# Another order of the loads ahead of and in the first 17 steps of an attention and two-layer-MoE kernel on one core

## The chip, the cores and the metric

The kernel runs on one core of one Trainium2 chip. The metric is the device time of one execution in microseconds (us); lower is better. The core has TensorE (PE, matrix products), VectorE (DVE), ScalarE (ACT), GpSimd (POOL) and SyncE (SP), which here only issues transfers. Each engine works through its own list of instructions in the order in which the program gave them, and waits at an instruction until what it needs is there.

## What is computed

```python
scores = scale * (q @ k.T)                       # 4 batches, 8 heads, 576 tokens, head size 64
scores = where(mask, scores, -1e9)               # 4 heads local (32 back), 4 heads strided (every 32nd)
x = softmax(scores) @ v                          # -> 2304 tokens x 512
h = x @ w_in;  x = (h * cos(h)) @ w_out          # first MoE layer, 512 -> 2048 -> 512
h = x @ w_in2                                    # second layer, the same sizes
g = (a0 + a1*h + a2*h**2 + a3*h**3) / (1 + |b0|*|h| + |b1|*h**2 + 1e-6)
out = g @ w_out2
```

The weights come as 64-bit floats and are decoded on the chip.

## The kernel before

**Work and tiles.** Attention is cut into 8 halves `n` (batch and half of its tokens) by 4 pairs of heads `pr`. The first layer runs over 5 blocks of tokens (512, 352, 480, 480, 480 columns), each in 16 steps, one for each 128-wide slice `f` of the hidden layer; that makes steps 0 to 79. The second layer runs over 5 blocks of 384 or 512 tokens, steps 80 to 159. In step `g`, `l1` (L478) makes `h` for its slice with 12 matmuls, ACT and DVE make `h*cos(h)` of it (letters U or u, V, N, M, G, H or h of `ew_op`), and `l2` (L495) adds the slice of step `g-2` into the output banks `y` with 12 matmuls (9 or 12 in the second layer). Each product is made of a high and a low part: `w_split` makes a weight tile's high part (ACT, L260) and its low part (DVE or POOL, L263); `att_oe` (L456, L457) does the same for attention's result, `xh` and `xl`.

**The start.** The halves 0 and 1 of attention are computed ahead of step 0, in the order of the list START, a line for each piece: `lq` and `lv` load q with k, and v; `load i j` loads a weight tile (a `raw` of 128 x 1024 words, 512 KB); `s` scores; `red` and `exps`, or `ms` and `ex`, two ways to the softmax (`exps` is five ACTIVATE with their sums, `ex` a single one); `t`, `te`, `o`, `oe` transpose, copy, multiply by v, split; `abs`, `d`, `split` decode a weight tile (ACT L233, L238; DVE L248, L250, L252, L254) and split it. A command has its engine or bank behind it.

**Queues.** Loads go through the queue of SP, a few of START through that of ACT. An issue waits until the transfer eight places before it in the program has landed, and until its buffer is free; all behind it in that queue wait too.

**The steps.** The other halves of attention ride along with steps 0 to 63. PAIR tells for each of them (key -4 is half 2, pair 0) the steps of: load q, load v, scores, masked maximum, exp, sum and reciprocal, transpose, product with v. W1LD tells the step whose end loads the weight tiles of pairs 6 to 15 of the first layer. The decoding of pair k begins in step k-3. ORD[g] is the order, letter by letter, of what ACT, DVE and POOL get in step g. W2T tells when a tile of the second layer's weights is decoded and stored back to memory; W2RD tells how many steps after step 64+f the two tiles of slice f, read back, are split (the third number is how many steps earlier they are read).

```python
            if g < N1:
                run("pe", g)                      # attention's matmuls of this step, behind l1
                for c in order(g): ...            # ORD[g]
                second(g, LAG)                    # l2 of step g-2
            run("load", g)                        # loads of this step, behind all of it
```

Of the kernel before, what the change touches and what calls it, by code (L numbers as in the profile page):

```python
# [88 lines left out]
ORD = {0: 'UVNykMaz1bpqGsHW23O4E',
 1: 'U1VSOyENz2MWb34aGpkqh',  # L90
 2: 'SOUEwzVNbyq1MaGkH234p',
 3: 'ykUzVwEN1SbOaMqp23G4h',
 4: 'Ey1USakVzwNbM2pGqO3H4',
 5: 'Uk1VwSObNMzy2q3EGaph4',
 6: 'yuVWskzN1ME2pqabGOH34',
 7: 'zUVwSN1yaMkp23EqObG4h',
 8: 'O1sUVwEzkNMaqGbH2y34p',
 9: 'UsH1OVy2bEWzap3G4qNMk',
 10: 'UkEbVyWGz1pNOM2q34has',
 11: 'yUsVN1az2EM3WGkOHqbp4',  # L100
 12: 'zb1ywkOG23SEUaMV4pqNh',
 13: 'UzaMVys1bqpE23NOW4kGH',
 14: 'byE1UpzMks2a3VOqNWG4H',
 15: 'zk1SMypUVObwGaHN234qE',
 16: 'Ud1EMkeVGO2r3Nfi4H',
 17: 'udekOfiMVGrEN12h34',
# [19 lines left out]
 37: 'kUVENM1dGhefOi234r',  # L126
 38: 'kUVE1NMdGOefi23h4r',
 39: 'kUVENMdG1Oefi23h4r',
 40: 'kUVENM1dGOefi234hr',
 41: 'kUVENM1OdGefi234hr',  # L130
 42: 'kUVENM1OdGefi234hr',
# [9 lines left out]
 52: 'UMdkV1ENGef2Hi34rO',
 53: 'MdkUVN1EGef23rHi4O',
 54: 'UVMk1dENGefi2H34rO',
 55: 'kuVM1dENGefi2h34rO',
 56: 'kuVM1dENGefi2h34rO',
 57: 'kuVM1d2ENGefih34rO',
 58: 'kuVM1d2ENGefih34rO',
 59: 'kuVM1d2ENGefih34rO',
 60: 'kuVM1d2ENGefih34rO',
 61: 'kuVM1dENGef2hO34ri',  # L150
 62: 'uVENM1kdGefiO234Hr',
 63: 'kuVM1dNGeEfi2HO34r',
# [9 lines left out]
 73: 'kUEV1MdNGefO2i3hr4',
 74: 'kUEV1MdNGefO2i3hr4',
 75: 'kUEV1MdNG2efOi34hr',
 76: 'kUEV1MGNdef2i34hrO',
 77: 'kUEV1MGNOdefi234hr',
 78: 'kU1MVNdEOGefi234Hr',
 79: 'UMNVEd1kOGefi234hr'}
START = ['cst ACT', 'lq 0 0 ACT', 'lq 0 1', 'lq 0 3 ACT', 'lv 0 0 ACT', 'lv 0 3 w0 ACT', 'lv 0 2 w0', 'lq 1 1 w1', 'lq 0 2 ACT', 'lq 1 0 w1', 'lq 1 3 w1 ACT', 'lq 1 2 w1 ACT', 'lv 1 0 w0 ACT', 'load 0 0',
# [777 lines left out]
```

## Time and profile before

| | us |
|---|---|
| three runs, median (lowest to highest) | 922.94 (922.39 to 923.59) |
| the profiled execution, its own time | 923.4 |
| its span, first to last instruction | 921.6 |
| PE busy in it | 891.8 (97%) |
| DVE busy | 661.9 (72%) |
| ACT busy | 624.5 (68%) |
| POOL busy | 239.1 (26%) |

A timeline row has its start, its duration, engine, line of the kernel, instruction, tile written and tiles read, and in brackets how long the engine had been idle and what released it. Matmuls overlap: a row of one lasts longer than the distance to the next.

### The profile page before, as it was taken

What the parts mean: (1) busy time and instruction counts of PE and PEld (TensorE: products, weight loads), DVE (VectorE), ACT (ScalarE), POOL (GpSimd) and SP (SyncE); (2) the same over time, 40 slices, a digit from 0 to 9 for tenths busy, and PEclk for the clock granted to TensorE, in tenths of its full rate; (3) what the DMA queues carried; (4) which work ended last, traced back from release to release, by engine and by line L of the source; (5) the groups of instructions that cost most, each with busy time, mean ns of one, the idle gap of its engine ahead of it and who ended that gap; (6) DMA issues with size and microseconds to landing.
All of it is one profiled execution on the core that took longest, in us unless ns stands there. A gap on an engine that the chain in (4) does not pass through costs nothing.

```text
span 921.6 us, 14207 instructions
## 1 busy us (share of the span) xinstructions
PE 891.8 (97%) x5263; PEld 760.9 (83%) x5263; DVE 661.9 (72%) x1162; ACT 624.5 (68%) x1106; POOL 239.1 (26%) x203
## 2 busy tenths in 40 slices
PE   8599999999999999999999999999999999999998
PEld 7477777999888887888888889888888888888986
DVE  5689985767685665576356798777777677767776
ACT  4789976667557555423355889777777777777775
POOL 0133553221321112201221124233223322332221
PEclk9799999999999999999999999999999999999999
DMA  9983041665644444231323340020011002000100
GB/s 274 325 280 135 8 154 56 203 206 163 185 131 155 154 120 147 95 109 51 97 87 116 102 131 1 1 80 1 0 53 40 1 1 80 1 1 1 46 1 35
DMA packets 54677, 88.16 MB, mean 96 GB/s; under 512 B 9544, under 2 KB 30800, under 8 KB 54608
## 3 DMA queue, kind: packets, MB, share of 16 engines
q1 hardware_dynamic: 51596, 83.64, 28.5%
q10 hardware_dynamic: 3012, 3.62, 1.3%
...
## 4 chain that ended last, share of the span: by engine, by line
PE 81%; DMA 7%; ACT 6%; DVE 4%; issue 1%; SPq 0%; ACTq 0%; POOL 0%; DVEq 0%
PE y L495 39%; PE h L478 27%; PE a L478 10%; DMA raw<-in_w_dram 3%; PE a L335 2%; DMA v<-in_vv_dram 2%; PE a L443 2%; PE a L421 1%; DMA qk<-in_qk_dram 1%; DMA ab<-in_a_dram 1%; ACT dec L233 1%; DVE w L263 1%; ACT w L260 1%; ACT gh L570 1%; ACT raw L238 1%
## 5 line engine op out<-in xcount | busy, mean ns | idle before, releaser
L478 PE MATMUL h<-xh,w 128*128 128x480 f32 (+3 forms) x960 | 296.6, 370 | 4.2 <-ACT w L260 2.6
L495 PE MATMUL y<-gh,w 128*128 128x480 f32 (+2 forms) x640 | 205.0, 382 | 0.0
L478 PEld LDWEIGHTS h<-xh,w 128*128 128x128 f32 x960 | 178.9, 188 | 30.0 <-DVE u L567 2.9
L495 PE MATMUL y<-w,gh 128*128 128x512 f32 x576 | 190.7, 390 | 1.3 <-ACT ev L510 1.3
L478 PE MATMUL h<-xl,w 128*128 128x480 f32 (+3 forms) x480 | 178.5, 372 | 0.0
L537 POOL TENSOR_TENSOR z<-q,r 128x512 f32<-128x512 f32 (+1 forms) x80 | 94.7, 1184 | 279.8 <-ACT r L536 276.9
L495 PEld LDWEIGHTS y<-gh,w 128*128 128x128 f32 x640 | 120.3, 190 | 18.6 <-issue 0.3
L495 PEld LDWEIGHTS y<-w,gh 128*128 128x128 f32 x576 | 108.1, 188 | 23.7 <-ACT ev L510 1.6
L495 PE MATMUL y<-gl,w 128*128 128x480 f32 (+2 forms) x320 | 119.9, 375 | 0.2 <-DVE gl L572 0.2
L495 PE MATMUL y<-w,gl 128*128 128x512 f32 x288 | 113.0, 392 | 0.7 <-DVE gl L550 0.5
L526 DVE SCALAR_TENSOR_TENSOR q<-q,z 128x512 f32<-128x512 f32 (+1 forms) x80 | 52.7, 659 | 84.4 <-ACT z L524 84.4
L478 PEld LDWEIGHTS h<-xl,w 128*128 128x128 f32 x480 | 90.6, 189 | 13.0
L478 PE MATMUL a<-xh,w 128*128 128x512 f32 (+1 forms) x320 | 98.2, 367 | 0.0
L565 ACT ACTIVATE u<-u,biases 128x480 f32<-128x480 f32 (+2 forms) x80 | 54.4, 680 | 61.3 <-DVE u L563 60.3
L559 ACT ACTIVATE u<-h,biases 128x480 int32<-128x480 f32 (+2 forms) x64 | 40.9, 638 | 78.9 <-PE h L478 78.9
L563 DVE SCALAR_TENSOR_TENSOR u<-h,u 128x480 f32<-128x480 f32 (+2 forms) x80 | 50.9, 636 | 55.1 <-ACT u L559 54.2
L572 POOL TENSOR_TENSOR gl<-u,gh 128x480 fp32r<-128x480 f32 (+2 forms) x31 | 40.5, 1306 | 147.4 <-ACT gh L570 130.4
L495 PEld LDWEIGHTS y<-gl,w 128*128 128x128 f32 x320 | 61.0, 191 | 8.5 <-DVE gl L572 0.7
L478 PEld LDWEIGHTS a<-xh,w 128*128 128x128 f32 x320 | 59.4, 188 | 8.1
L495 PEld LDWEIGHTS y<-w,gl 128*128 128x128 f32 x288 | 54.1, 188 | 12.7 <-DVE gl L550 2.2
L570 ACT ACTIVATE gh<-u 128x480 fp32r<-128x480 f32 (+2 forms) x80 | 46.2, 577 | 20.8 <-DVE u L567 20.6
L478 PE MATMUL a<-xl,w 128*128 128x512 f32 (+1 forms) x160 | 59.1, 369 | 0.0
(126 smaller groups left out, 1455.0 us busy)
## 6 DMA issues: line engine op xcount, KB each, us to landing
...
```

The lines of the kernel that those rows point to most:

```text
L233: ACT.activation(out=m, in_=src, func=AF.Copy, scale=2.0 ** -112)
L335: PE.matmul(sv[r, i], t[r, q0:q0 + D], rhs[r], start=not mask, stop=not mask or i == nb - 1)
L443: PE.matmul(o[64 * j:64 * j + 64, q * i:q * i + m], v[0:w, i, 64 * j:64 * j + 64], r[i][0:w, 64 * j:64 * j + m], start=True, stop=True)
L478: PE.matmul(h[:, :n], w[d["ph"], f, 0][:, 128 * c:128 * c + 128], x[c][:, cs], start=k == 0, stop=k == len(ops) - 1)
L495: PE.matmul(y, l, r, start=first and i == 0, stop=last and i == 2)
L526: DVE.scalar_tensor_tensor(out=q, in0=q, scalar=1.0 + 1e-6, in1=z, op0=ALU.add, op1=ALU.add)
L537: POOL.tensor_tensor(out=z, in0=q, in1=r, op=ALU.mult)
L559: ACT.activation(out=k, in_=h, func=AF.Identity, scale=INV_2PI, bias=biases[:, 2:3])
L563: DVE.scalar_tensor_tensor(out=u, in0=h, scalar=INV_2PI, in1=k, op0=ALU.mult, op1=ALU.subtract)
L565: ACT.activation(out=u, in_=u, func=AF.Sin, scale=TWO_PI, bias=biases[:, 3:4])
L570: ACT.activation(out=e["gh"], in_=u, func=AF.Copy)
L572: (POOL if c == "H" else DVE).tensor_tensor(out=e["gl"], in0=u, in1=e["gh"].bitcast(F32), op=ALU.subtract)
```

## The change

It replaces the tables: START, PAIR, W1LD, W2RD, W2T, ORD, the two default orders AB_ORD and C_ORD, and M3 (one more weight tile is decoded with two DVE instructions in place of one on DVE and one on ACT). A new table WHE sends both parts of four splits of the second layer's weights to named engines. No transfer, no matmul and no tile is added or taken away; in START six sets of scores instead of four go through `red` and `exps`.

```diff
-W2RD = (5, 7, 2)
+W2RD = (2, 4, 2)
-PAIR = {-4: (1, 1, 2, 3, 5, 6, 8, 9),
- -3: (1, 5, 5, 5, 5, 8, 10, 11),
- -2: (4, 10, 5, 7, 10, 10, 12, 13),
- -1: (7, 12, 9, 9, 10, 12, 14, 15),
- 0: (8, 10, 11, 11, 14, 15, 16, 18),
+PAIR = {-4: (1, 1, 3, 3, 5, 6, 8, 9),
+ -3: (3, 4, 5, 5, 5, 8, 10, 11),
+ -2: (0, 8, 6, 7, 10, 10, 12, 13),
+ -1: (7, 14, 9, 9, 10, 12, 14, 15),
+ 0: (6, 11, 11, 11, 13, 13, 16, 18),
...
-W1LD = [0, 3, 0, 4, 5, 6, 6, 6, 10, 11]
-M3 = [(9, 0), (3, 0)]
+W1LD = [2, 3, 0, 3, 6, 6, 3, 6, 3, 9]
+M3 = [(9, 0), (3, 0), (14, 1)]
+WHE = {(2, 3, 0): "POOL", (2, 3, 1): "POOL", (2, 5, 0): "DVE", (2, 5, 1): "DVE"}
...
-ORD = {0: 'UVNykMaz1bpqGsHW23O4E',
+ORD = {0: 'uVWNykMpazbq1GHS23EO4',
...
- 'te 1 3', 'd 0 1 1', 'o 1 3 h', 'd 0 1 2', 'oe 1 2', 'split 0 1 DVE', 'oe 1 3', 'd 1 1 1', 'abs 1 0', 'load 4 0',
- 'd 1 0 1', 'oe 1 1', 'split 0 0 DVE', 'd 1 0 2', 'd 1 1 2', 'next', 'split 1 0 DVE', 'split 1 1 DVE', 'load 5 0', 'load 5 1']
+ 'o 1 2 a', 'd 0 0 2', 'oe 1 1', 'te 1 3 DVE', 'o 1 3 y', 'split 0 1 POOL', 'd 1 1 1', 'abs 1 0', 'd 1 0 1', 'split 0 0 POOL',
+ 'oe 1 2', 'oe 1 3', 'next', 'd 1 0 2', 'd 1 1 2', 'split 1 0 DVE', 'load 5 0', 'split 1 1 POOL', 'load 5 1', 'load 4 0']
...
     def w_split(m, key, f, o, eng, heng=None):
+        heng = heng and dict(POOL=POOL, DVE=DVE)[heng]
...
-                    w_split(raws.pop(("f", f, o)), 2, f, o, DVE)
+                    w_split(raws.pop(("f", f, o)), 2, f, o, DVE, WHE.get((2, f, o)))
```

(The rows of lists that show `...` hold more lines of the same kind. Lines of code from L257 on stand one or two places further down in the changed kernel.)

**SP's queue in START.** The rows before; the last `v` of 63x5x128 x2 is that of half 1, pair 3, which `o 1 3`, the last piece of attention ahead of step 0, waits for:

```order
L224 DMA raw<-in_w_dram 128x1024 x3
L302 DMA v<-in_vv_dram 63x5x128 x2
L302 DMA v<-in_vv_dram 96x5x128
L224 DMA raw<-in_w_dram 128x1024 x2
L781 DMA ab<-in_a_dram 128x4
L782 DMA ab<-in_b_dram 128x2
L302 DMA v<-in_vv_dram 96x5x128
L224 DMA raw<-in_w_dram 128x1024 x3
L302 DMA v<-in_vv_dram 63x5x128 x2
L224 DMA raw<-in_w_dram 128x1024 x7
```

and with the change:

```order
L225 DMA raw<-in_w_dram 128x1024 x2
L304 DMA v<-in_vv_dram 96x5x128
L783 DMA ab<-in_a_dram 128x4
L784 DMA ab<-in_b_dram 128x2
L225 DMA raw<-in_w_dram 128x1024 x3
L304 DMA v<-in_vv_dram 96x5x128
L304 DMA v<-in_vv_dram 63x5x128 x2
L225 DMA raw<-in_w_dram 128x1024 x2
L304 DMA v<-in_vv_dram 63x5x128 x2
L225 DMA raw<-in_w_dram 128x1024 x4
```

Eight `raw` stand ahead of that `v` before and seven after; the tiny `ab` loads and a `v` have moved up. A ninth `raw`, on ACT's queue, is program-wise ahead of it before and behind it after.

**SP's queue for steps 5 to 12.** Before, from the eight `raw` of steps 5 and 6 on:

```order
L224 DMA raw<-in_w_dram 128x1024 x8
L274 DMA qk<-in_qk_dram 128x962 x2
L302 DMA v<-in_vv_dram 63x5x128
L302 DMA v<-in_vv_dram 96x5x128
L224 DMA raw<-in_w_dram 128x1024 x4
```

and with the change, from the eight `raw` of step 3 on:

```order
L225 DMA raw<-in_w_dram 128x1024 x8
L304 DMA v<-in_vv_dram 96x5x128
L276 DMA qk<-in_qk_dram 128x962
L225 DMA raw<-in_w_dram 128x1024 x6
L276 DMA qk<-in_qk_dram 128x962
L304 DMA v<-in_vv_dram 63x5x128
L225 DMA raw<-in_w_dram 128x1024 x2
L304 DMA v<-in_vv_dram 96x5x128
L225 DMA raw<-in_w_dram 128x1024
```

Before, two loads of `v`, which wait for a buffer that attention's products of steps 9 and 11 free, stand ahead of the last four `raw` (pairs 14 and 15). Now pair 14 is loaded in step 3, and one `v` stands ahead of the two `raw` of pair 15; but six `raw` (pairs 10, 11, 13) have a `qk` ahead of them.

**ACT from the last pieces of START into step 0.** Before; `w_632` is the weight tile that step 0 multiplies with, `xh_86<-h` the last piece of attention, `u<-h,biases` of 128x512 letter U of step 0:

```order
L260 ACTIVATE w_618<-dec 128x512
L456 ACTIVATE xh_86<-h 128x32x9
L233 ACTIVATE dec<-raw 128x512
L238 ACTIVATE raw<-raw 128x512
L456 ACTIVATE xh_84<-y 128x288
L260 ACTIVATE w_632<-dec 128x512
L233 ACTIVATE dec<-raw 128x512 x2
L238 ACTIVATE raw<-raw 128x512
L260 ACTIVATE w_642<-dec 128x512
L260 ACTIVATE w_645<-dec 128x512
L559 ACTIVATE u<-h,biases 128x512
L565 ACT_TABLE_LOAD
```

and with the change:

```order
L262 ACTIVATE w_624<-dec 128x512
L234 ACTIVATE dec<-raw 128x512
L239 ACTIVATE raw<-raw 128x512
L262 ACTIVATE w_632<-dec 128x512
L458 ACTIVATE xh_85<-a 128x32x9
L458 ACTIVATE xh_86<-y 128x32x9
L234 ACTIVATE dec<-raw 128x512 x2
L239 ACTIVATE raw<-raw 128x512
L262 ACTIVATE w_646<-dec 128x512
L262 ACTIVATE w_651<-dec 128x512
L567 ACT_TABLE_LOAD
L567 ACTIVATE u<-u,biases 128x512
```

Step 0's `w_632` has moved from behind the last piece of attention (and a decode) to ahead of it, and U of step 0 has left ACT; it is letter u, on DVE. The low parts of three of the four tiles split in START have gone from DVE to POOL.

## Rows read from the trace of the kernel before

**Rows 1.** Page, part 1: busy time, share of the span, instructions
```profile
PE 891.8 (97%) x5263; PEld 760.9 (83%) x5263; DVE 661.9 (72%) x1162; ACT 624.5 (68%) x1106; POOL 239.1 (26%) x203
```

**Rows 2.** Stretches: width, busy of PE, PEld, DVE, ACT, POOL, clock, DMA share, GB/s
```profile
0.00:39.26 39.26, 28.59 (x420) 23.89 (x420) 22.40 (x60) 21.23 (x72) 6.15 (x10) 0.96 1.00 285
11.68:35.00 23.32, 19.47 (x315) 16.05 (x315) 18.01 (x47) 19.94 (x71) 5.94 (x6) 1.00 1.03 305
36.40:46.60 10.20, 4.78 (x28) 3.99 (x29) 5.23 (x9) 5.38 (x10) 0.00 (x0) 0.50 1.03 350
51.30:120.00 68.70, 66.07 (x396) 52.90 (x397) 65.36 (x111) 63.36 (x110) 32.49 (x24) 0.98 0.38 135
...
590.00:840.00 250.00, 250.00 (x1105) 207.07 (x1104) 187.05 (x283) 188.82 (x296) 74.02 (x59) 1.00 0.07 24
```

**Rows 3.** Timeline of PE, the rows with a long wait ahead
```profile
32.37 0.78 PE L443 MATMUL y<-pt,v 126*64 126x63 f32 x20
39.26 1.29 PE L443 MATMUL h<-pt,v 126*64 126x63 f32 x20 [6.11 <-DMA v<-in_vv_dram]
43.11 0.79 PE L478 MATMUL h<-xh,w 128*128 128x512 f32 x1 [2.57 <-ACT w L260]
...
51.32 0.50 PE L478 MATMUL h<-xh,w 128*128 128x512 f32 x1 [0.79 <-DVE u L567]
...
88.28 0.50 PE L478 MATMUL h<-xh,w 128*128 128x512 f32 x1 [0.85 <-DVE u L567]
...
92.59 0.56 PE L421 MATMUL a<-cst,p 128*89 128x128 f32 x3 [1.29 <-POOL p L412]
93.62 0.42 PE L421 MATMUL a<-cst,p 128*89 128x128 f32 x2 [0.47 <-DVE p L360]
...
124.01 0.43 PE L421 MATMUL a<-cst,p 128*63 128x128 f32 x2 [2.08 <-DVE xl L457]
...
528.87 0.50 PE L495 MATMUL y<-w,gh 128*128 128x512 f32 x1 [1.31 <-ACT ev L510]
```

**Rows 4.** Timeline of SP's queue, issues
```profile
29.01 0.74 SPq L302 DMA_DIRECT2D v<-in_vv_dram  x2
...
101.89 13.50 SPq L302 DMA_DIRECT2D v<-in_vv_dram  x2
115.49 1.86 SPq L224 DMA_DIRECT2D raw<-in_w_dram  x4
```

**Rows 5.** Chain that ended last, in order of time: start, us, what
```profile
94.05 4.34 PE y L495 x12
...
108.79 2.78 PE y L495 x12
...
124.44 4.58 PE y L495 x12
```

**Rows 6.** Timeline of ACT, end of START, step 0, step 11
```profile
40.58 0.66 ACT L456 ACTIVATE xh<-h 128x288 fp32r<-128x288 f32 x1 [5.58 <-PE h L443]
...
42.43 0.63 ACT L260 ACTIVATE w<-dec 128x512 fp32r<-128x512 f32 x1
...
48.53 1.28 ACT L565 ACT_TABLE_LOAD   x1
...
120.92 0.66 ACT L233 ACTIVATE dec<-raw 128x512 f32<-128x512 f32 x1 [1.62 <-DMA raw<-in_w_dram]
```

**Rows 7.** Groups of ACT by line, 11 to 35 us: busy us, mean ns
```profile
L369 ACT ACTIVATE p<-p 128x445 f32<-128x445 f32 (+2 forms) x4 | 2.4, 596 | 9.8 <-DVE mx L383 9.7
...
L392 ACT ACTIVATE p<-h,mx 128x89 f32<-128x89 f32 x5 | 1.6, 331 | 0.0
```

**Rows 8.** Low parts of splits by engine, 50 to 130 us: ns lowest, median, highest
```profile
L263 DVE TENSOR_TENSOR w<-dec,w x12: 650/698/1117, 54.5 to 128.3; 128x512 fp32r<-128x512 f32 x12
L263 POOL TENSOR_TENSOR w<-dec,w x12: 1293/1498/1757, 60.3 to 126.6; 128x512 fp32r<-128x512 f32 x12
```

**Rows 9.** Waits of PE: waiting line, what ended it, us in total, times, longest
```profile
PE a L335 <- DVE p L360: 4.0, 5, 1.2
```

More of the change, by code (lines that the diff above doesn't have):

```diff
@@ L78 @@
  18: (45, 50, 47, 47, 50, 50, 52, 53),
[1 row of a table removed]
-W2T = [(14, 16, 17, 17, 17), (14, 17, 17, 18, 18), (17, 19, 19, 20, 20), (18, 20, 20, 21, 22), (21, 23, 23, 24, 24), (21, 23, 24, 24, 24), (23, 25, 25, 26, 26), (26, 27, 27, 28, 28), (25, 27, 27, 28, 28),
[3 rows of a table removed]
-W1LD = [0, 3, 0, 4, 5, 6, 6, 6, 10, 11]
-M3 = [(9, 0), (3, 0)]
[1 row of a table added]
+W2T = [(14, 16, 17, 17, 17), (13, 17, 17, 18, 18), (17, 19, 19, 20, 20), (18, 20, 20, 21, 22), (21, 23, 23, 24, 24), (21, 23, 24, 24, 24), (23, 25, 25, 25, 26), (26, 27, 27, 28, 28), (25, 27, 27, 28, 28),
[3 rows of a table added]
+W1LD = [2, 3, 0, 3, 6, 6, 3, 6, 3, 9]
+M3 = [(9, 0), (3, 0), (14, 1)]
+WHE = {(2, 3, 0): "POOL", (2, 3, 1): "POOL", (2, 5, 0): "DVE", (2, 5, 1): "DVE"}
 TED = []
 AB_ORD = "UNW1V2MyzH3SkEGapOb4q"
-C_ORD = "MdkEUVN1Gef23rOHi4"
-ORD = {0: 'UVNykMaz1bpqGsHW23O4E',
[L90 to L106, printed above, removed]
+C_ORD = "1ukVdMGeNf2EH3iOr4"
+ORD = {0: 'uVWNykMpazbq1GHS23EO4',
+ 1: 'zU1VOySNwab234EMkpqGh',
+ 2: 'EOSkUzwVNbyq1pMaGH234',
+ 3: 'yzkUwVN1SO2EMqb3p4aGh',
+ 4: 'Uky1saVzwEN2bMGpO3H4q',
+ 5: 'EkU1VwbNMzSO2q3yGph4a',
+ 6: 'ykuVsWzN12EpMqabOGH34',
+ 7: 'UzwaEVSN1yM2kp3qbOG4h',
+ 8: 'sUOVwEzNMaGqkb1yH234p',
+ 9: 'UsVH1ObEy2Wzap3G4NqMk',
+ 10: 'UEVW1bGyzpNqOM23k4has',
+ 11: 'ysEuVNa1zW2MGHkOpb34q',
+ 12: 'zbUy1Wk2ap3S4MGVOhENq',
+ 13: 'zUMVas1yE2NGHOpqb34wk',
+ 14: 'yz1EpbMS2k3GWOU4aVHNq',
+ 15: 'skUz1yMbVOW2aqGhp34EN',
+ 16: 'O1dEeMGH23urfiVN4k',
+ 17: 'rduVeMOGfNhEik1234',
  18: 'kUVMENdefGiO123r4h',
@@ L109 @@
  20: 'UVk1ENMdOGefi23r4h',
- 21: 'UVk1ENrMdGhefi2O34',
+ 21: 'UVkENr1MdGhefi2O34',
  22: 'MdkUEVN1Gef23rOHi4',
@@ L125 @@
  36: 'kUVENM1dGOefi234rh',
[L126 to L131, printed above, removed]
+ 37: 'kUVENM1dGhe2fOi34r',
+ 38: 'kUVE1NM2dGO3efih4r',
+ 39: 'kUVENMdG1Oefi23rh4',
+ 40: 'kUVENM12dGOefi3r4h',
+ 41: 'kUVENM12OdGefi3r4h',
+ 42: 'kUVENM1OdGefi23r4h',
  43: 'kUVENM1GOdefi234rh',
  44: 'kUVENMO1dGefi234rh',
- 45: 'kUVENM1GOdefi234hr',
+ 45: 'kUVENMG1Odef2i34hr',
  46: 'kUVENM1GOdefi234hr',
- 47: 'kUVENM1OdGefi234hr',
+ 47: 'kUVMEN1OdGefi234hr',
@@ L137 @@
  48: 'kU1VENMdGefiO234rH',
- 49: 'kUV1ENMdGefi234OHr',
- 50: 'kUMV1ENdGefi234Ohr',
+ 49: 'kOUV1ENMdGefi234Hr',
+ 50: 'kOUMV1ENdGefi234hr',
  51: 'kUVM1ENdGefiO234rh',
[L141 to L152, printed above, removed]
@@ L153 @@
- 64: 'ku1VMdeENGfi2HO34r',
- 65: 'ku1VMdENGefi2HO34r',
+ 52: 'MUkV1dNEGHef23i4rO',
+ 53: 'dkMUVNG1ef2E3Hri4O',
+ 54: 'uVMkN1dEef2G3h4irO',
+ 55: 'UVkM1dENG2efi3h4rO',
+ 56: 'kUdVM1NEG2efi3h4rO',
+ 57: 'kUdVM12ENGefi3h4rO',
+ 58: 'kUVM1d2ENGefi3h4rO',
+ 59: 'kUVM1d2ENGefih34rO',
+ 60: 'kUVM1d2ENGefih34rO',
+ 61: 'kUVM1dENeGf2hO34ri',
+ 62: 'UVENM1kdGefiO234Hr',
+ 63: 'kuVM1dENGefi2HO34r',
+ 64: 'ku1VMdGeENfi2HO34r',
+ 65: 'ku1VMdeENGOfi2H34r',
  66: 'kUMVE1NdGefi2O34rH',
- 67: 'ku1VMdEGefN2HO3r4i',
@@ L157 @@
- 68: 'kUEV1NMdGefiO234rH',
- 69: 'ku1VMdENGefi2HO34r',
- 70: 'ku1VMENdGefi2HO34r',
+ 67: 'kU1VMdEGefN2HO3r4i',
+ 68: 'kuEV1NMdGefiO234rH',
+ 69: 'ku1VMdGeENOfi2H34r',
+ 70: 'ku1VMENdGeHfi2O34r',
  71: 'kUEV1MdNGefiO234hr',
  72: 'kUEV1MdNGefiO234hr',
[L162 to L169, printed above, removed]
[7 rows of a table removed]
+ 73: 'kuV1NMdGef2iO3hr4E',
@@ L177, in attention_moe_moe_kernel @@
+ 74: 'UV1MdNGef2i3hr4OkE',
+ 75: 'uV1MdeNG2fOi34hrkE',
+ 76: 'uV1MGNdef2i34hrOkE',
+ 77: 'UEV1MdGNOefi234hkr',
+ 78: 'kU1MVNGdEOefi234Hr',
+ 79: 'NUMVEd1kOGefi234hr'}
+START = ['cst ACT', 'lq 0 3 ACT', 'lq 0 1', 'lq 0 0 ACT', 'lv 0 0 ACT', 'lv 0 3 w0 ACT', 'lv 0 2 w0', 'lq 0 2 ACT', 'lq 1 0 w1', 'lq 1 1 w1', 'lq 1 2 w1 ACT', 'lv 1 0 w0 ACT', 'warm 38', 'lq 1 3 w1 ACT',
[7 rows of a table added]
 @with_exitstack
@@ L683, in split1 @@
         if k < len(d):
-            w_split(d[k][1][1], 1, *d[k][0], eng)
+            w_split(d[k][1][1], 1, *d[k][0], eng, WHE.get((1, *d[k][0])))
     def order(g):
@@ L830, in do @@
                 elif op == "split":
-                    w_split(ms[n[0], n[1]][1], 1, *pairs[n[0]][n[1]], eng, engs[1])
+                    w_split(ms[n[0], n[1]][1], 1, *pairs[n[0]][n[1]], eng, WHE.get((1, *pairs[n[0]][n[1]])))
                 elif op == "t":
```

29 rows, old and new, of tables (PAIR, START, W2T) are left out of this document.

## The prediction

> **What bounds the kernel now.** I read first the busy times of the page, then the same by stretches, then the timeline of PE for every long wait, and at each wait the timeline of the engine that ended it. PE is busy for 891.8 of 921.6 us [rows 1], and from 590 to 840 us for every one of the 250 us [rows 2]: there its matmuls alone set the time. The matmuls stay as they are, so an engine made faster there gives nothing, and what can be won is PE's idle time and the time that it works at the lower clock. A shift won early lasts to the end if nothing later gives it back.
>
> Almost all of it lies ahead of 130 us. PE sits idle for 6.11 us until 39.26 for a load of `v`, and for 2.57 us more until step 0 starts at 43.11 [rows 3]. The load of `v` is issued only at 29.01 to 29.75 [rows 4]. From 0 to 39.26 the transfers keep their engines busy all the time (share 1.00) at 285 GB/s [rows 2]: the `v` is late because of the bytes ahead of it, not because of its issue. From 36.4 to 46.6 the granted clock is 0.50, the lower of its two levels, 1.2 instead of 2.4 GHz [rows 2]. Later PE waits 0.79 us at 51.32, then 0.85, 1.29 and 0.47 us between 88 and 94, and 2.08 us at 124.01 [rows 3]. After the last two groups twelve matmuls of `l2` take 4.34 and 4.58 us where they else take 2.78 [rows 5]: 1.6 and 1.8 us more. From 51.3 to 120 DVE is busy for 65.36 and ACT for 63.36 of 68.70 us [rows 2], so there the vector engines are nearly as full as PE.
>
> **The parts of the change, each against the profiled execution's own 923.4 us.**
>
> *The start.* Ahead of the last `v` one `raw` of 512 KB leaves SP's queue and another, on ACT's queue, comes behind it: 1.05 MB less. At 285 GB/s [rows 2] that is 3.7 us, so the `v` would land at about 35.6 instead of 39.26. ACT then becomes the one to watch. From 11.68 to 35 it is busy for 19.94 of 23.32 us, so it idles for 3.4 [rows 2], and after the `v` it still works from 40.58 to 43.06, 2.5 us [rows 6], up to the split that step 0 waits for. Two more sets of scores go through `exps`: 1.6 us of ACT in place of one ACTIVATE of 0.6 us [rows 7], twice, so 2.0 us more. With the old idle time ACT would be through at 35.0 + 2.5 + 2.0 = 39.5, with none of it at 36.1. Step 0's split now stands ahead of the last piece of attention, so the 2.57 us no longer come behind the `v`, but in its shadow. I take a start of step 0 at 38.0, between the two ends and nearer to the later, since ACT keeps its waits for PE and DVE: 43.11 - 38.0 = **5.1 us**. The bounds are 2.6 (the `v` lands as before, and only the second wait goes) and 7.0 (ACT without idle time).
>
> The low parts of three splits that moved to POOL take 1.5 us there instead of 0.7 on DVE [rows 8]. Step 0 needs its own only for its last four matmuls, so I cost that at nothing; without that cover it is 0.8 us.
>
> *Step 0's cosine.* u is on DVE, and so the table load of 1.28 us [rows 6] no longer stands between U and the sine. PE's wait of 0.79 us at 51.32 [rows 3] should go: **0.8 us**. The bounds are 0, and 2.0 if the lower clock no longer falls on steps 0 and 1.
>
> *Waits between 88 and 94.* PE waits for a multiplication that DVE does late, then for POOL, which waits for a sum on DVE. Counted in the order of DVE, two low parts fewer stand between step 0 and that sum: 2 x 0.7 = 1.4 us [rows 8]. The three waits are 2.61 us, and the lower clock behind them costs 1.6 more [rows 5]. The single wait of 1.31 us at 528.87 [rows 3] has no lower clock behind it, so a rest of about 1.2 may have none either. With DVE at 95% I don't count on all of it: **2.2 us**, between 0 and 4.2.
>
> *The wait at 124.* ACT waited 1.62 us until 120.92 for a `raw` [rows 6], one of the four that were issued at 115.49, behind two loads of `v` that held the queue from 101.89 on [rows 4]. In the new order two of these four are loaded in step 3, and the other two wait for one `v` only, whose buffer comes free at about 101.89. That is 13 us sooner, so ACT's wait should go, and with it PE's 2.08 us and the 1.8 us of lower clock: up to 3.9. I take **2.9 us**, as something else may come late in those steps; the bounds are 0 and 3.9.
>
> *The second layer's weights, split sooner.* Three steps sooner means that some six splits leave steps 80 to 86, where PE waited 1.31 us for ACT to empty an output bank [rows 3]: **0.8 us**, between 0 and 1.3. What covers them now is steps 66 to 79, in which PE alone sets the pace.
>
> *New orders in steps 1 to 17 and 52 to 79.* No row shows them. Five waits of PE for DVE's masked maximum, 4.0 us in all [rows 9], lie where the order hardly changes, and they stay. With DVE and ACT as full as they are, new waits of the kind of the old ones are likely. I take **-1.5 us**, two of the middle size; the bounds are +1 and -5, the size of the two largest stalls with their clock.
>
> The sum: 5.1 + 0.8 + 2.2 + 2.9 + 0.8 - 1.5 = 10.3 us, so 913.1. The profiled execution lies 0.5 us above the median of the three runs, 922.94; against that it is 912.6.
>
> **The rivals.**
>
> *The start alone (B).* DVE and ACT give the middle back: they are full from 51.3 to 120 [rows 2], and earlier steps only make PE wait for them elsewhere. Then 5.1 + 0.8 + 0.8 - 1.5 = 5.2 stay: 917.7. For it: two low parts fewer is little in 68 us. Against it: PE's waits there came from late sums and a late `raw`, both of which the new order touches.
>
> *POOL in DVE's way (C).* In rows the two disturb each other in part: DVE's low part has a median of 698 ns and a highest of 1117, while POOL works beside it [rows 8], so some 0.4 us for each; three in the start cost 1.3 us at most. If a DVE instruction waited instead for all of POOL's 1.5 us, three of them just ahead of and in step 0 would take 4.5 us of the 5.1, and DVE's relief at 88 would be gone: 0.6 + 0.8 + 2.9 + 0.8 - 1.5 = 3.6, so 919.3. The Trainium skill ("SBUF — State Buffer", section "Who interferes with whom") says just that: a DVE instruction with two inputs in SBUF and a GpSimd instruction that reads SBUF exclude each other for the whole instruction. The highest of 1117 ns speaks for something between.
>
> *Nothing at the end (E).* The transfers move as many bytes in the first 60 us as before, and the start is paid back when the next weights come late: 922.9.
>
> *Slower (D).* Six `raw`, pairs 10, 11 and 13, now stand behind a `qk` that waits until PE has made the scores of step 6. ACT starts to decode pair 10 in step 7. If the `qk` and the `raw` land after that, ACT stops as it did at 120.92, and each time PE pays 2.08 us and 1.8 us of clock [rows 3, 5]. Two such stops are 7.8 us; with the middle lost too it is 5.1 + 0.8 + 0.8 - 1.5 - 7.8 = -2.6, so 925.5. It decides at the distance between step 6's scores and ACT's turn in step 7, two groups of twelve matmuls or some 5.5 us at 2.78 each [rows 5], against 1.5 MB, 5.3 us at 285 GB/s [rows 2]. It speaks against it that 285 GB/s holds for the crowded start, and the queue is emptier in step 6.
>
> **How the numbers follow.** My forecast (A), with its own range of 907 to 916, has 0.45; B 0.27, C 0.12, E 0.10, D 0.06. The likeliest is A, 912.6. The range of 8 in 10 takes in A, B and C up to 920, and at the low end the larger gains of the start and of the waits, 906. Two tenths of a percent, 1.8 us, is about what a measurement of this kernel can tell from no change. Faster by more than that are A, B and C: 0.84; within it E: 0.10; slower D: 0.06.
>
> **What would show it.** In the profile after, the wait of PE for `v` ends at about 36 and step 0 starts at 37 to 39; ACT has no longer a wait of 5 us in the start. PE has no wait of 0.79 us ahead of step 2's `l1`. The wait of 2.08 us in step 12 is gone, and no `raw` is awaited there. The clock is 1.00 from 50 us on. The wait at the empty output bank in step 83 is under 0.6 us. The prediction is wrong if step 0 starts after 41, if the last `v` still lands at 39, or if ACT waits for a `raw` in steps 7 to 10.

## The result, and the profile after the change

| | before | changed |
|---|---|---|
| median of 4 runs (lowest to highest), us | 922.66 (922.30 to 923.59) | 912.03 (911.53 to 912.89) |
| profiled execution, its own time / span, us | 923.4 / 921.6 | 911.99 / 910.2 |
| ratio, with its 95% interval | | 0.9884 (0.9867 to 0.9901) |

The forecast was 912.6. The medians differ by 10.6 us, the profiled pair by 11.4. Busy times and stretches of the changed kernel, against [rows 1] and [rows 2] (columns as there):

```profile
PE 890.3 (98%) x5263; PEld 760.5 (84%) x5263; DVE 658.2 (72%) x1162; ACT 623.9 (69%) x1118; POOL 242.0 (27%) x207
```

```profile
0.00:36.00 36.00, 28.94 (x395) 23.41 (x395) 17.45 (x55) 21.58 (x87) 5.57 (x10) 0.95 1.00 284
36.00:42.40 6.40, 6.12 (x51) 5.06 (x52) 5.70 (x9) 5.15 (x10) 2.56 (x2) 0.50 1.00 396
47.50:116.00 68.50, 66.18 (x400) 52.59 (x401) 65.32 (x111) 64.55 (x113) 35.33 (x26) 1.00 0.55 190
...
590.00:840.00 250.00, 250.00 (x1110) 207.88 (x1109) 186.58 (x283) 187.19 (x295) 73.22 (x58) 1.00 0.07 23
```

PE works 1.5 us less than before and idles 9.9 us less (span less busy time). From 47.5 us on the granted clock is 1.00 up to the tail; the two dips behind the waits of [rows 3] at 94 and 124 are gone. From 590 to 840 us nothing changed. PE's long waits, as in [rows 3]:

```profile
35.98 1.33 PE L423 MATMUL h<-cst,p 128*126 128x128 f32 x5 [2.05 <-DVE p L414]
38.81 1.29 PE L445 MATMUL y<-pt,v 126*64 126x63 f32 x20 [0.28 <-DVE pt L434]
47.56 0.50 PE L480 MATMUL h<-xh,w 128*128 128x512 f32 x1 [0.68 <-DVE u L569]
51.23 0.50 PE L497 MATMUL y<-gl,w 128*128 128x512 f32 x1 [0.44 <-POOL gl L574]
...
84.76 0.50 PE L480 MATMUL h<-xh,w 128*128 128x512 f32 x1 [0.25 <-DVE u L569]
88.75 0.56 PE L423 MATMUL a<-cst,p 128*89 128x128 f32 x3 [0.96 <-POOL p L414]
89.69 0.45 PE L423 MATMUL a<-cst,p 128*89 128x128 f32 x2 [0.38 <-DVE p L362]
...
117.67 0.43 PE L423 MATMUL a<-cst,p 128*63 128x128 f32 x2 [0.71 <-DVE xl L459]
...
518.85 0.50 PE L497 MATMUL y<-w,gh 128*128 128x512 f32 x1 [0.65 <-ACT ev L512]
```

The 6.11 us for `v` and the 2.57 us for step 0's split have gone; 2.05 us for DVE have come (35.98), and 0.28 us (38.81) is all that is left where PE used to wait for `v`. The 2.08 us of 124 are 0.71. SP's queue shows why, against [rows 4]:

```profile
20.52 1.23 SPq L304 DMA_DIRECT2D v<-in_vv_dram  x3
21.80 1.39 SPq L225 DMA_DIRECT2D raw<-in_w_dram  x2
23.23 2.85 SPq L304 DMA_DIRECT2D v<-in_vv_dram  x2
...
96.40 0.30 SPq L304 DMA_DIRECT2D v<-in_vv_dram  x1
96.81 0.81 SPq L225 DMA_DIRECT2D raw<-in_w_dram  x2
109.57 0.33 SPq L304 DMA_DIRECT2D v<-in_vv_dram  x1
```

The last two pieces of `v` are issued at 23.23 to 26.08 in place of 29.01 to 29.75, and at 96.81 two `raw` go out 13 us before the second `v` gets its buffer (109.57), in place of behind it.

**Where the gain arises.** PE does the same products in the same order of steps, so its position can be compared. The table has the us by which a kernel's profiled execution is ahead of the profiled execution of before, at the first `l1` of step 0 and at the start of `l2` of five steps (PE's timeline). Attention's pieces ride in other steps in the two kernels, so single steps up to 15 jump by some 0.8 us; the chosen ones lie outside of such jumps. The runs of the lower rows follow below.

| ahead of before by, us | step 0 `l1` | `l2` 5 | `l2` 7 | `l2` 11 | `l2` 70 | `l2` 86 |
|---|---|---|---|---|---|---|
| (before: it starts at) | 43.11 | 84.5 | 102.5 | 133.2 | 474.8 | 555.4 |
| changed | 3.1 | 2.9 | 5.5 | 8.0 | 9.3 | 11.4 |
| changed, another execution (c_after) | 4.1 | 3.5 | 6.1 | 8.6 | 9.9 | 12.0 |
| START alone (e1_start) | 3.9 | 3.7 | 3.7 | 6.3 | 5.4 | 5.6 |
| all but START (e4_rest) | -0.2 | -1.4 | 1.2 | 3.9 | 5.6 | 7.6 |
| steps 0 to 36 alone (e10_mid) | 0.5 | -0.1 | 2.6 | 5.3 | 5.4 | 5.8 |
| second weights alone (e3_late) | 0.3 | 0.5 | 0.4 | 0.5 | -0.2 | 1.8 |
| two pairs' loads alone (e2_w1ld) | -2.1 | -2.2 | -2.2 | 1.1 | 0.7 | 0.9 |

Read along the row "changed": 3.1 us come before step 0, none in steps 0 to 5, 2.6 around 88 to 94, 2.5 around 124, 1.3 from there to step 70, 2.1 in the first steps of the second layer.

### The profile page after: what moved, and what is told of

It reads as the page before. It is cut to its first block, busy times and chain, and to the rows that moved or that the text cites. A ratio compares the mean times of both kernels' runs of the same rounds, so it can differ in the third digit from the quotient of the medians.

```text
span 910.2 us, 14217 instructions
## 1 busy us (share of the span) xinstructions
PE 890.3 (98%) x5263; PEld 760.5 (84%) x5263; DVE 658.2 (72%) x1162; ACT 623.9 (69%) x1118; POOL 242.0 (27%) x207
## 4 chain that ended last, share of the span: by engine, by line
PE 81%; ACT 7%; DVE 5%; DMA 4%; issue 1%; SPq 1%; POOL 0%; ACTq 0%; POOLq 0%; DVEq 0%
PE y L497 39%; PE h L480 27%; PE a L480 10%; DMA qk<-in_qk_dram 3%; PE a L337 2%; PE a L445 1%; PE a L423 1%; DMA raw<-in_w_dram 1%; ACT dec L234 1%; ACT w L262 1%; DVE dec L249 1%; ACT raw L239 1%; DVE w L265 1%; ACT gh L572 1%; DVE dec L251 1%
## 5 line engine op out<-in xcount | busy, mean ns | idle before, releaser
L497 PE MATMUL y<-gh,w 128*128 128x480 f32 (+2 forms) x640 | 202.9, 378 | 0.0
L574 POOL TENSOR_TENSOR gl<-u,gh 128x480 fp32r<-128x480 f32 (+2 forms) x29 | 37.6, 1298 | 122.5 <-ACT gh L572 114.1
L497 PEld LDWEIGHTS y<-w,gl 128*128 128x128 f32 x288 | 54.1, 188 | 11.4 <-DVE gl L552 1.0
L414 POOL TENSOR_TENSOR p<-p,sm 128x445 f32<-128x445 f32 (+2 forms) x24 | 27.3, 1139 | 124.6 <-DVE sm L408 124.6
```

Of the source, the lines that this page charges most:

```text
L414: mul.tensor_tensor(out=pv, in0=pv, in1=sm[:, 8:8 + NBLK].unsqueeze(2).to_broadcast([128, NBLK, w]), op=ALU.mult)
L497: PE.matmul(y, l, r, start=first and i == 0, stop=last and i == 2)
L574: (POOL if c == "H" else DVE).tensor_tensor(out=e["gl"], in0=u, in1=e["gh"].bitcast(F32), op=ALU.subtract)
```

## The experiments

Each run has the kernel before as its measure on the same chip; its medians were 922.26 (23 runs, beside e1 to e4), 921.74 (9, beside e5 to e8) and 922.19 us (17, beside the last four). The changed kernel itself ran for the result and as c_after, but not on the chip of e5 to e8: these four are set against it by their ratios to before (0.9884 and 0.9879 for the changed kernel).

| run | median, us (runs) | ratio to before, 95% interval |
|---|---|---|
| e1_start | 916.88 (6) | 0.9948 (0.9931 to 0.9966) |
| e2_w1ld | 921.35 (12) | 0.9995 (0.9984 to 1.0006) |
| e3_late | 920.87 (12) | 0.9982 (0.9968 to 0.9995) |
| e4_rest | 915.02 (6) | 0.9931 (0.9915 to 0.9948) |
| e5_U | 910.45 (4) | 0.9879 (0.9863 to 0.9894) |
| e6_dve | 910.66 (4) | 0.9878 (0.9865 to 0.9892) |
| e7_norm | 911.56 (4) | 0.9888 (0.9874 to 0.9901) |
| e8_v | 912.64 (5) | 0.9906 (0.9889 to 0.9923) |
| c_after | 911.46 (4) | 0.9879 (0.9863 to 0.9895) |
| e9_late_raw | 910.38 (4) | 0.9871 (0.9852 to 0.9891) |
| e10_mid | 918.66 (12) | 0.9966 (0.9952 to 0.9980) |
| e11_best | 913.10 (4) | 0.9895 (0.9878 to 0.9911) |

### The parts alone: START, the rest, the middle, the end

e1_start, the kernel before with

```diff
-START = [... of before]
+START = [... of the changed kernel]
```

> The kernel before with the new START alone; every table for step 0 and later is the old one. The changed kernel started step 0 at 40.0 us in its trace, 3.1 earlier than before. Theory (the terms of the sum stand each at its own place and add up): step 0 starts at 40.0 here too, the waits at 88 to 94 and at 124 stay, and the time is 922.7 - 3.1 = 919.6 us. Rival (DVE and ACT are full from step 0 to step 12, so an early start only makes PE wait for them): step 0 at 40.0, but the waits up to 130 us grow by what was won, and the time is 921.5 to 922.7.

5.4 us by the medians, more than either side expected. Step 0 is 3.9 us ahead, and nothing of that is given back up to step 7: the rival falls. The waits around 88 stay as they were, so they don't hang on START. The surplus arises at 124, where half of the wait goes as well. PE, ACT and SP's queue of this run:

```profile
88.88 0.56 PE L423 MATMUL a<-cst,p 128*89 128x128 f32 x3 [1.32 <-POOL p L414]
...
119.28 0.43 PE L423 MATMUL a<-cst,p 128*63 128x128 f32 x2 [1.06 <-DVE xl L459]
```

```profile
116.18 0.68 ACT L234 ACTIVATE dec<-raw 128x512 f32<-128x512 f32 x1 [0.59 <-DMA raw<-in_w_dram]
```

```profile
98.18 13.49 SPq L304 DMA_DIRECT2D v<-in_vv_dram  x2
```

The two `v` hold the queue as in [rows 4], and ACT still waits for a `raw` ahead of PE's 1.06 us, but for 0.59 us in place of 1.62 [rows 6], and the granted clock no longer falls behind it. (A second such wait, 0.94 us at 120.79, comes behind PE's and holds up nothing on PE.) ACT had its `raw` 4.40 us after the queue was free again at 111.78; before, it took 5.43 us from 115.49. Why it came faster is open. Of the 2.6 us won there, 0.9 are given back by step 70.

e4_rest, the changed kernel with

```diff
-START = [... of the changed kernel]
+START = [... of before]
```

> The changed kernel with the START of before. Theory (the terms add up): step 0 starts at 43.1 again, everything behind is as in the changed kernel, and the time is 912.0 + 3.1 = 915.1 us. Rival (the relief of DVE at 88 and 124 comes in part from the splits that START gives to POOL, so it goes with it): the waits at 88 and 124 are back in part and the time is 916.5 to 918 us.

915.02: the terms add up, and the rival falls. The two kernels together (5.4 and 7.2 us) make 12.6 where the change makes 10.6, since each of them contains a gain at the stall at 124. The 1.2 us that its trace loses in steps 0 to 5 stand beside a lower clock that lasts until 48.4 us, 5.1 us into step 0, where before it was 3.5. Around 88 PE's waits are those of the changed kernel, though START's four low parts are on DVE here:

```profile
89.05 0.50 PE L480 MATMUL h<-xh,w 128*128 128x512 f32 x1 [0.25 <-DVE u L569]
93.04 0.56 PE L423 MATMUL a<-cst,p 128*89 128x128 f32 x3 [0.98 <-POOL p L414]
93.97 0.45 PE L423 MATMUL a<-cst,p 128*89 128x128 f32 x2 [0.38 <-DVE p L362]
```

e10_mid, the kernel before with

```diff
-PAIR, W1LD, M3, ORD[0] to ORD[36]: of before
+PAIR, W1LD, M3, ORD[0] to ORD[36]: of the changed kernel
```

> The kernel before with the new PAIR, W1LD and orders of steps 0 to 36 alone; START and the second layer's splits are the old ones. Theory (in the trace with the old START, step 20 gained 4.4 us, 1.2 of them around 88 to 94 and 2.7 at 124): 4 to 5 us less than before, 917.2 to 918.5 us where before is 922.3; no lower clock in steps 8 and 12. Rival (the loads moved to step 3 push START's last transfers back, as one look with two of them moved showed the v 2 us later): step 0 at 45 us and 919.5 us or more.

918.66, 3.5 us less, just above the theory's 917.2 to 918.5. In the trace 2.7 us come around 88 and 2.7 at 124, no clock dip follows either, and step 0 starts at 42.63, so the rival falls. The waits at 88 follow a sum that DVE comes to late. The low parts of splits on DVE between step 2's `l1` and that sum, before and in this run:

```profile
L263 DVE TENSOR_TENSOR w<-dec,w x7: 681/702/1045, 54.5 to 85.6; 128x512 fp32r<-128x512 f32 x7
```

```profile
L265 DVE TENSOR_TENSOR w<-dec,w x5: 679/682/830, 54.6 to 84.7; 128x512 fp32r<-128x512 f32 x5
```

Seven before and five here. There are five in e4_rest and in the changed kernel too, which have the gain, and seven in e1_start, e2_w1ld and e3_late, which haven't. The two moved with the tables of the steps, not with START.

e3_late, the kernel before with

```diff
-W2RD, W2T, WHE, ORD[37] to ORD[79]: of before
+W2RD, W2T, WHE, ORD[37] to ORD[79]: of the changed kernel
```

> The kernel before with the new tables for the second layer's weights (when they are decoded, read back and split, and on which engine) and the new orders of steps 37 to 79. Theory (in the changed kernel the steps 80 to 87 gained 2.0 us and steps 40 to 70 about 1.1): the waits at 528.9 and 542.8 shrink or go, and the time is 919.7 to 920.7 us. Rival (only what was forecast for the splits, 0.8 us, belongs to them, and the rest came from earlier steps' shifts): 921.9 us.

1.4 us less by the medians, a little short of the theory. From step 70 to step 86 it gains 2.0 us, as the changed kernel does. The 0.7 us that it loses before step 70 come with waits at 289.62 and 290.52 (0.49 and 0.22 us) that neither whole kernel has; the cut at step 37 makes them. In the second layer PE's second wait of before was this one, and DVE just ahead of it:

```profile
541.72 0.50 PE L495 MATMUL y<-w,gh 128*128 128x512 f32 x1
542.76 0.50 PE L495 MATMUL y<-w,gl 128*128 128x512 f32 x1 [0.54 <-DVE gl L550]
```

```profile
537.80 1.40 DVE L263 TENSOR_TENSOR w<-wf,w 128x512 fp32r<-128x512 f32 x2 [1.08 <-ACT w L260]
...
542.15 0.55 DVE L550 TENSOR_TENSOR gl<-a,gh 128x384 fp32r<-128x384 f32 x1
```

Two low parts of splits (1.40 us) stand in DVE's chain up to the `gl` that PE waits for. In e3_late and in the changed kernel this wait is gone, and the one at the output bank is halved:

```profile
528.45 0.50 PE L497 MATMUL y<-w,gh 128*128 128x512 f32 x1 [0.64 <-ACT ev L512]
```

### The stall at 124: which edit removes it

e2_w1ld, the kernel before with

```diff
-W1LD = [0, 3, 0, 4, 5, 6, 6, 6, 10, 11]
+W1LD = [0, 3, 0, 4, 5, 6, 6, 6, 3, 9]
```

> The kernel before with only the loads of pairs 14 and 15 moved, from steps 10 and 11 to steps 3 and 9. Theory (PE's 2.08 us at 124 come from the raw that was issued late): ACT's wait of 1.62 us for a raw and PE's wait of 2.08 us are gone, with the lower clock behind them, so 2.7 to 3.9 us: 919 to 920 us. Rival (something else is late in the same steps, or the raw moved ahead push q, k or v back): under 1 us, 921.7 to 922.7 us.

In its trace the stall is gone: 3.3 us from step 7 to step 11, PE's wait 0.39, and the two `v` stand behind the `raw` in SP's queue.

```profile
124.51 0.43 PE L423 MATMUL a<-cst,p 128*63 128x128 f32 x2 [0.39 <-DVE xl L459]
```

```profile
98.82 4.34 SPq L225 DMA_DIRECT2D raw<-in_w_dram  x2
104.08 13.50 SPq L304 DMA_DIRECT2D v<-in_vv_dram  x2
```

But the medians are only 0.9 us apart, and the interval takes in no change; the lowest of the twelve, 920.02, is 2.2 us under the median of before. The profiled execution, the slowest of the twelve (922.46), lost 2.1 us ahead of step 0, where the program is that of before: the last `v` came at 41.32.

```profile
41.32 1.29 PE L445 MATMUL h<-pt,v 126*64 126x63 f32 x20 [6.77 <-DMA v<-in_vv_dram]
```

So the place is settled by the trace, the total isn't: whether the start was late in all twelve, and why, stays open. e10_mid moves the same two pairs with more, and its start wasn't late.

e9_late_raw, the changed kernel with

```diff
-W1LD = [2, 3, 0, 3, 6, 6, 3, 6, 3, 9]
+W1LD = [2, 3, 0, 3, 6, 6, 3, 6, 10, 11]
```

> The changed kernel with the loads of pairs 14 and 15 back at steps 10 and 11. Theory (the late raw made the stall at 124, and these two numbers took it away): ACT waits for a raw in step 11 again, PE waits 2 us or more at the place where it now waits 0.71 (117.67), the granted clock falls behind it, and the time is 1.4 to 3.2 us above the changed kernel beside it. Rival (the earlier start or the other v order alone had removed it): PE's wait there stays under 1 us, the time within 0.7 us of the changed kernel.

The theory falls: PE's wait is 0.67, the time 910.38 beside 911.46. SP's queue says why:

```profile
95.21 0.30 SPq L304 DMA_DIRECT2D v<-in_vv_dram  x1
103.16 0.80 SPq L225 DMA_DIRECT2D raw<-in_w_dram  x2
108.37 0.33 SPq L304 DMA_DIRECT2D v<-in_vv_dram  x1
```

The new PAIR asks for one `v` in step 8 and the next in step 11, so no pair of `v` stands ahead of the `raw` of step 10, and these go out at 103.16, where before it was 115.49. Other steps for the `raw` alone take the stall away (e2_w1ld), and so do other steps for the `v` together with the new START (e9_late_raw), which by e1_start takes half of it. The queue is what these edits have in common. The new PAIR without the new START and without the new W1LD was not run.

### What sets the start now

c_after, the changed kernel itself.

> The changed kernel once more, as the measure for the three that run beside it, and for how far its start varies from one execution to the next. 911 to 912.5 us; step 0 between 39 and 41 us.

Step 0 at 39.05 here, at 40.03 in the first profile. The five profiled executions with the new START and nothing else changed ahead of step 0 (changed, c_after, e1_start, e5_U, e9_late_raw) have 40.03, 39.05, 39.26, 37.41 and 38.36, mean 38.8; the five with the old one (before, e2_w1ld, e3_late, e4_rest, e10_mid) 43.11, 45.18, 42.79, 43.28 and 42.63, mean 43.4. START is worth 4.6 us by these means, 3.1 in the first pair. In e5_U and e9_late_raw the granted clock stayed at 1.00 here; the other three, in which it fell as it did in all five old ones, have a mean of 39.4, so 4.0 us at a like clock.

DVE of the changed kernel in these microseconds:

```profile
30.03 0.81 DVE L379 TENSOR_REDUCE early<-p 128x5 f32<-128x630 f32 x1 [1.10 <-ACT p L371]
...
33.33 0.16 DVE L407 TENSOR_SCALAR early<-early 128x5 f32<-128x5 f32 x1
...
35.12 0.81 DVE L414 TENSOR_TENSOR p<-p,early 128x630 f32<-128x630 f32 x1
...
38.20 0.89 DVE L434 COPY pt<-h 126x384 f32<-126x384 f32 x2 [0.70 <-PE a L445]
39.01 2.33 DVE L249 SCALAR_TENSOR_TENSOR dec<-dec,raw 128x512 int32<-128x512 int32 x2
```

The last softmax has its sum at 30.84 and its product only from 35.12 on: two decode instructions, four low parts of attention and a copy stand in between on DVE, with hardly a pause. PE waits for this product (35.98), not for the `v`.

e8_v, the changed kernel with

```diff
- 'lv 1 3 w0', 'load 2 1',
+ 'load 2 1', 'lv 1 3 w0',
```

> The changed kernel with the last v (half 1, pair 3) one raw further back in SP's queue, so eight raw ahead of it as in the kernel before. 512 KB are some 1.8 us at 285 GB/s, so it lands at about 37.1 in place of 35.3. Theory (in the changed kernel the v is there before it is needed at 38.8): step 0 at 40.0, 912.0 us. Rival (the v still ends the start): PE waits for it, step 0 at 41.5 or later and 913.5 us or more.

Between the two. PE waits 1.04 us for the `v`, which comes at 38.73; step 0 starts at 39.96. What the one `raw` alone costs the `v` isn't shown: the trace of the changed kernel has no landing time for it, and in this execution SP's queue was 1.5 us late already ahead of the edit (three `v` issued at 22.05, in the changed kernel at 20.52).

```profile
38.73 1.29 PE L446 MATMUL y<-pt,v 126*64 126x63 f32 x20 [1.04 <-DMA v<-in_vv_dram]
```

e6_dve (below), on the same chip and with the `v` in its new place, has step 0 at 38.90 and 910.66 us, this run 912.64; its five times lie at 912.02 or above, those of e5_U, e6_dve and e7_norm at 912.02 or below. In the changed kernel the `v` no longer ends the start, but one `raw` more ahead of it makes it do so.

e7_norm, the changed kernel with

```diff
- 'ex 1 3', 't 1 1 h', 'sum 1 3', 'oe 0 2', ... 'rec 1 3', 'oe 0 3', ... 'te 1 2', 'norm 1 3 DVE',
+ 'ex 1 3', 't 1 1 h', 'sum 1 3', 'rec 1 3', 'norm 1 3 DVE', 'oe 0 2', ... 'oe 0 3', ... 'te 1 2',
```

> The changed kernel with the reciprocal and the multiplication of half 1, pair 3 (rec 1 3, norm 1 3) right behind its sum on DVE; in the changed kernel two decode instructions, three low parts and a copy stood between them, and PE waited 2.05 us for the product at 35.98. Theory (it is this order on DVE, no longer the v, that sets the start of step 0): PE's wait is under 0.8 us, step 0 starts at 38.3 to 38.8 and the time is 910.3 to 910.8 us; if the granted clock then doesn't fall at 35.6, up to 1.5 us less. Rival (the v's landing or ACT's decoding sets the start): step 0 at 39.5 to 40, the time 911.5 to 912 us.

The wait of 2.05 us is gone, and others stand in its place:

```profile
33.93 0.80 PE L446 MATMUL y<-pt,v 89*64 89x58 f32 x20 [0.91 <-DVE pt L435]
37.94 0.78 PE L446 MATMUL y<-pt,v 126*64 126x63 f32 x20 [1.81 <-DVE pt L435]
39.01 0.50 PE L481 MATMUL h<-xh,w 128*128 128x512 f32 x1 [0.29 <-ACT w L263]
```

Step 0 at 39.01, 911.56 us: nothing won, and the time is the rival's. DVE's next copy comes late in place of the product, and the last wait, 0.29 us, is for ACT's split of step 0's own tile. So with this order DVE and ACT end within 0.3 us of each other. That the amount of their work sets the start, and not some other order, fits this but is argued.

### Step 0's cosine, and POOL's low parts

e5_U, the changed kernel with

```diff
-ORD = {0: 'uVWNykMpazbq1GHS23EO4',
+ORD = {0: 'UVWNykMpazbq1GHS23EO4',
```

> The changed kernel with step 0's U back on ACT (one letter). Theory (u on DVE is worth the ACTIVATE that it takes from the chain in front of the sine, some 0.6 us): PE's wait ahead of step 2's l1 grows from 0.68 to about 1.3 us, and the time is 912.6 us. Rival (step 0's chain waits for the sine's table load whichever engine makes u): the wait stays at 0.7 us and the time at 912.0 us.

PE's wait ahead of step 2's `l1` is 1.05 us. The changed kernel has 0.44 and 0.68 at the lower clock; at 1.00, as here, e9_late_raw has 0.81. So the wait grows the theory's way, by 0.24 us at a like clock in place of 0.6. The time, 910.45, shows no loss. In this execution the granted clock was 1.00 all through the start, and PE waited for DVE all the same:

```profile
39.97 0.50 PE L480 MATMUL h<-xl,w 128*128 128x512 f32 x1 [1.12 <-DVE xl L459]
45.73 0.50 PE L480 MATMUL h<-xh,w 128*128 128x512 f32 x1 [1.05 <-DVE u L569]
```

e6_dve, the changed kernel with

```diff
- 'split 0 1 POOL', ... 'split 0 0 POOL', ... 'split 1 1 POOL',
+ 'split 0 1 DVE', ... 'split 0 0 DVE', ... 'split 1 1 DVE',
```

> The changed kernel with the three low parts that START gives to POOL back on DVE. Theory (DVE is the full engine, each low part costs it 0.7 us, and POOL disturbs it by 0.4 us at most for each): some 0.3 us times three come later on DVE in steps 0 to 8, the waits of PE at 84 to 90 us grow, and the time is 912.7 to 914 us. Rival (POOL's low part holds DVE for its whole length, 1.3 us): DVE is through earlier without it, PE's wait ahead of step 2's l1 gets shorter, and the time is 911.2 to 912 us.

910.66 us, no loss and no clear gain; PE's waits at 84 to 90 are unchanged, so the theory falls, and the wait ahead of step 2's `l1`, 0.45, lies within the 0.44 to 0.68 of the changed kernel. The two kernels' decodes that stand beside POOL's low parts, DVE of e6_dve, then POOL of the changed kernel:

```profile
38.48 1.28 DVE L250 SCALAR_TENSOR_TENSOR dec<-dec,raw 128x512 int32<-128x512 int32 x2
```

```profile
37.27 1.28 POOL L265 TENSOR_TENSOR w<-dec,w 128x512 fp32r<-128x512 f32 x1 [7.88 <-ACT w L262]
38.92 1.27 POOL L265 TENSOR_TENSOR w<-dec,w 128x512 fp32r<-128x512 f32 x1 [0.36 <-ACT w L262]
```

Two decodes take 1.28 us without POOL and 2.33 beside it (the row at 39.01 above). POOL's second low part began at 38.92 and ended at 40.19; the pair of decodes began at 39.01 and ended 1.15 us after that, nearly their whole length. So one of three low parts held DVE for 1.05 us and the other two for nothing that shows, against 3 x 0.68 us taken off DVE. In the six other traces whose START has these low parts on POOL the pair meets one as well: 2.37 us in c_after and e1_start, 2.57 to 2.79 in e5_U, e7_norm, e8_v and e9_late_raw, so DVE is held for 1.1 to 1.5 us each time.

### A version with more waits removed

e11_best, the changed kernel with

```diff
START: 'rec 1 3', 'norm 1 3 DVE' behind 'sum 1 3'; 'd 0 0 2' ahead of 'd 0 1 2'; 'split 0 0 DVE', 'split 0 1 DVE'
- 15: 'skUz1yMbVOW2aqGhp34EN',  31: 'UVk1MENdOeGfi23h4r',
+ 15: 'skUOz1yMbVW2aqGhp34EN',  31: 'UOVk1MENdeGfi23h4r',
- 33: 'kUVEN1dMGOefi234rH',  47: 'kUVMEN1OdGefi234hr',
+ 33: 'kUOVE1NdMGefi234rH',  47: 'kUOVMEN1dGefi234hr',
```

> The changed kernel with the last pieces of START in another order on DVE (product of half 1, pair 3 right behind its sum; step 0's own weight decoded ahead of step 1's; its low parts on DVE) and with attention's split (letter O) ahead of the masked maximum in steps 15, 31, 33 and 47, as step 49 already has it, where PE waited 0.2 us in place of 0.65. Theory (each wait has its own place and they add up): step 0 0.5 to 1.3 us earlier; PE's waits of 0.66, 0.77, 0.65 and 1.26 us at 139, 224, 237 and 327 shrink to 0.2, 2.5 us less: 2.5 to 3.8 us under the changed kernel beside it, 908.2 to 909.5 us. Rival (O ahead of V makes the cosine late, and PE waits for gl or h instead): 0 to 1 us less.

913.10, no better than the 911.46 beside it. The profiled execution is the lowest of the four (911.20), with the clock at 1.00 up to the tail; the others are at 913.0 to 913.2. Step 0 starts at 37.29, at that clock hardly ahead of e5_U's 37.41, but the cosine behind it comes later, and three of the four waits grew or stayed. Two of its rows:

```profile
46.11 0.50 PE L481 MATMUL h<-xh,w 128*128 128x512 f32 x1 [2.14 <-DVE u L570]
...
138.39 0.65 PE L338 MATMUL a<-qk 64*64 64x126 f32 x8 [1.53 <-DVE xl L460]
```

At 139, 224, 237 and 327 the waits of 0.66, 0.77, 0.65 and 1.26 us became 1.53, 1.28, 0.21 and 1.27: with O first, PE waits for attention's split in place of the masked maximum. No version here beats the changed kernel by what a measurement can tell.

## Why the prediction was right, step by step

| term | forecast (bounds) | profiled pair |
|---|---|---|
| start up to step 0 | 5.1 (2.6 to 7.0) | 3.1; 4.6 by the means of five traces each |
| step 0's cosine, up to step 5 | 0.8 (0 to 2.0) | -0.2 |
| waits at 88 to 94 with their clock | 2.2 (0 to 4.2) | 2.6 |
| stall at 124 with its clock | 2.9 (0 to 3.9) | 2.5 |
| second weights split sooner | 0.8 (0 to 1.3) | 2.1 |
| new orders | -1.5 (+1 to -5) | +1.3 |
| sum | 10.3 | 11.4 |

**The reading of the bound held.** All of the gain is PE's idle time and its time at the lower clock: 8.0 of the 11.4 us ahead of 133 us, 1.3 from there to step 70, 2.1 where splits crowd the second layer. That the total is near is in part luck, since terms that are off in both directions cancel: the start and the cosine were forecast 3.0 us too high, the second weights and the new orders 4.1 too low. Three terms (the cosine, the second weights, the new orders) lie outside their bounds.

**The start: right in where, wrong in what is late next.** The `v` was issued 6 us sooner and is no longer waited for. ACT was named as the engine to watch; PE's waits of 2.05 and 0.28 us are for DVE, busy for 5.75 of the 6 us from 30 to 36 us in the changed kernel. ACT is nearly as full there (5.49), and in e7_norm the last wait is for it. The step that failed is the one that laid the new end of the start on ACT's idle time without the same sum for DVE.

**The cosine: the term failed.** The wait at 51.32 was to vanish; at its place 0.68 us stand (47.56), and 0.44 us for POOL's `gl` are new (51.23). u on DVE does shorten the wait, by 0.24 us (e5_U); with the other new tables beside it the wait falls from 0.79 to 0.43 (e10_mid), but not to nothing: the wait ends with a multiplication on DVE, not with the table load alone. The wait for `gl` comes with the new tables; e5_U, with U on ACT, has it too (0.43).

**The waits at 88 to 94: right in size, the reason borne out but not isolated.** They shrank from 2.61 to 1.59 us, and the larger part is the clock that no longer falls (the 1.6 us of [rows 5]). The reason given, two low parts fewer on DVE, agrees with the count: five in place of seven in every trace with the new tables of steps 0 to 36, which all have the gain, and seven in those without, which have none. START's low parts don't matter here: e4_rest has them on DVE and keeps the gain, e1_start has them on POOL and none. The same tables also change the order of the letters, and that wasn't taken apart from the two low parts.

**The stall at 124: right in mechanism and size.** It was the pair of `v` ahead of the `raw` in one queue. That the loads of the `raw` alone are enough (e2_w1ld), and those of the `v` too, with the other tables and the new START (e9_late_raw), was not seen; the prediction named both as one.

**The second weights: mis-sized.** 2.1 us against at most 1.3. The bound was read from the one wait at the output bank; the second one, 0.54 us for `gl` at 542.76, wasn't brought in, nor that the nine matmuls around it last longer than elsewhere (2.99 us from 541.72 to the next `l1` at 544.71, 2.08 in the changed kernel).

**The new orders: the sign was wrong.** New waits were expected on engines 95% full; what came (0.44 at 51.23, 0.24 at 111.11) is smaller than what went. Between steps 11 and 70 the waits of 0.43 us at 152.98 and 0.19 at 362.81 are gone, and of the five waits for the masked maximum, which were to stay, one fell from 0.65 to 0.20. The bounds leaned to the loss without a row for it.

**The rivals.** B (the start alone) falls: the middle kept its gains, in e4_rest even without the new START. E falls with it. C's mechanism exists, and is too small: e6_dve, which takes POOL out of DVE's way, has the changed kernel's ratio to before (0.9878 beside 0.9879 and 0.9884). The Trainium skill ("SBUF — State Buffer", section "Who interferes with whom") has a DVE instruction with both inputs in SBUF and a GpSimd instruction that reads SBUF exclude each other for the whole instruction. The traces agree for the pair of decodes that met a low part, held for 1.05 to 1.5 us; the copies and splits that ran beside the first low part, which read a bank that PE wrote, took their usual time (0.89 us for the copies at 38.20, 0.87 in e6_dve). D didn't happen: from 44 to 140 us ACT waits for no `raw` at all in the changed trace. Of the signs named beforehand three missed: step 0 at 40.03 us in place of 37 to 39, 0.68 us in place of none ahead of step 2's `l1`, 0.65 us in place of under 0.6 at the output bank.
